# Two attention and two feed-forward layers on one core: the K weights loaded in two column halves, the first K products split to match, and a new order

## The chip, the cores and the metric

The kernel runs on one core of one Trainium2 chip. The metric is the device time of one execution in microseconds. A profiled execution has a span, from its first to its last instruction, and a device time a little longer than that. The engines are TensorE (PE, with its weight loads shown apart as PEld), VectorE (DVE), ScalarE (ACT), GpSimd (POOL) and SyncE (SP), which issues all the DMAs here.

## The reference

The input x has 2048 rows of 512. Four residual layers follow: attention, feed-forward, attention, feed-forward, the two of each kind with the same weights.

```python
x = x + attn(layernorm(x), wqkv, wo)
x = x + ffn(layernorm(x), w1, w2)
x = x + attn(layernorm(x), wqkv, wo)
x = x + ffn(layernorm(x), w1, w2)

# attn: 32 heads of 16
q, k, v = split(x @ wqkv)
phi = lambda t: where(t > 0, t + 1, exp(t)) + 1e-6
kv  = einsum("bhsd,bhse->bhde", phi(k), v)
z   = einsum("bhsd->bhd", phi(k))
o   = (phi(q) @ kv) / (phi(q) . z + 1e-6)
out = o @ wo

# ffn: relu(x @ w1) @ w2, with 1376 hidden columns
```

## The kernel before

The 2048 rows are 16 tiles of 128 rows (one row per partition), and four tiles make a chunk. A layer's input is normalised tile by tile into `xn` (float16) and transposed into `Tb`, so that the 512 columns lie on partitions, in four blocks of 128. A K product of a tile (`kproj`, function `a_k`, L653) is four matmuls, one for each block, each 512 columns wide, into one PSUM bank; ACT then makes an exponential and a linear copy of it, and DVE joins the two to phi(k) (`phi_evac`, L610). A Q product is made transposed, four per chunk. For chunk 0 of layer 0 it is made in halves of two tiles, 256 columns wide (`a_q_half`, L735), and the evacuation follows the second half. G products (`a_g`) multiply xn with phi(k) over all rows; from G come the value part, the denominators and the matrix that the chunk's last products (`fin`) use. The feed-forward layers replace some products by sums and differences of blocks.

In layer 0, tiles of chunks 0 and 1 are transposed on PE (`transpose_pe`, L591: four 128-wide matmuls against an identity, then a copy to `Tb` on ACT or DVE); all the others are transposed by DMA, two tiles at a time (L586). The statistics of layer 0's tiles are made by DVE (L534, L535), the reciprocal root by ACT (tiles 0 to 3) or POOL, and the normalised tile by DVE (L572). From tile 2 on the statistics of a tile wait for the normalised tile two before it.

Before there is any input, PE runs eight matmuls on zeros (L503, `warm`). Behind the transposes of tiles 0 and 1 it runs four more each (`warm_fill`, L525 and L529), 128 columns wide; nothing reads their result.

All loads are issued by SP on one hardware queue, in the order of their priorities. Before: tile 0 of x, tile 1, tiles 2 and 3, wk (columns 512 to 1023 of wqkv, all 512 rows), chunk 1 of x, wq (columns 0 to 511), chunk 3, chunk 2, wv, one row of wv, wo, w1; w2 later. All chunks but the first few rows are read so that a partition holds consecutive rows.

The order of everything is planned by the program itself while it is built. Every operation is added to a graph with an assumed duration (`C_MM512` = 216 and so on) and, for a DMA, an assumed transfer time and lateness (`late`). `_list_schedule` (L200) then goes through the engines, each with a window of pending operations sorted by priority, and places the one that can start first. The priority is the operation's place in the program plus a number from the table `HINTS` (L55). An entry ending in `!` fixes which of several engines makes the operation. PSUM banks are handed out by the same planner. The order that comes out is written out as the instruction streams, each engine's in order, with semaphore waits where another engine or a DMA is waited for. The planner's times are only used to choose the order.

Steps of consecutive layers are interleaved: the next layer's step for a chunk begins as soon as its rows are ready, and the matmuls of both stand in one PE stream.

Of the kernel before, what the change touches and what calls it, by code (L numbers as in the profile page):

```python
# [16 lines left out]
C_MM512 = 216.0  # L17
# [37 lines left out]
HINTS = {"0.bnag8": 129, "0.bnst11": -246, "0.bnst12": 104, "0.bnst13": 129, "0.bnst14": 143, "0.bnst15": 144, "0.bnst6": -4,  # L55
# [276 lines left out]
def build_kernel(nc, A_x, A_wqkv, A_wo, B_w1, B_w2, out, n_layers_pairs=2, K_STT=0, Q_STT=0, windows=None,  # L332
# [20 lines left out]
    with es:  # L353
# [237 lines left out]
        def transpose_pe(i):  # L591
# [11 lines left out]
            if i < 2:  # L603
                warm_fill(i)
# [781 lines left out]
```

## Time and profile before

| | |
|---|---|
| median of 3 runs | 269.01 us (268.01 to 269.33) |
| profiled execution | 268.93 us, span 267.2 us |
| granted TensorE clock over the span, as recorded | 1.0 |
| PE busy | 262.0 us, 98% |
| DVE busy | 226.2 us, 85% |
| ACT busy | 187.0 us, 70% |
| POOL busy | 58.5 us, 22% |
| DMA | 22.18 MB, mean 83 GB/s |

In the profile L12 is line 12 of the kernel. A line of the chain gives start, length and what it was. A line of the timeline gives the start and the time from the first start to the last end of a run of like instructions (x4 is four of them), the engine, the line, the operation, what it writes and reads by the program's names, and its shape; in brackets the idle time before it and what ended that. PE rows include the drain of a matmul, which the next one overlaps, so a row of four matmuls is longer than four intervals. "DMA to landing" is the time from a DMA's issue to its completion.

### The profile page before, as it was taken

The page shows a single profiled execution, that of the slowest core. Times are in us where ns is not written, and L with a number is a line of the kernel's source. Part 1 is how long each engine was busy: PE and PEld are TensorE (multiplying, and loading weights), DVE is VectorE, ACT ScalarE, POOL GpSimd, SP SyncE. Part 2 cuts the span into 40 slices and gives each one's busy share as a digit, 9 for nine tenths or more (in the row PEclk, how much of TensorE's full clock was granted, in tenths as well). Part 3 has the DMA queues.
Part 4 walks back from the last instruction along what each step waited for, and adds up shares of the span by engine and source line. Part 5 has one row for each costly group of instructions (what it writes and reads, how often), then busy time and mean ns, then how long its engine had stood idle before and what let it go on. Part 6 is the DMA issues. An engine that isn't in the chain of part 4 may idle for free.

```text
span 267.2 us, 5481 instructions
## 1 busy us (share of the span) xinstructions
PE 262.0 (98%) x2020; PEld 183.1 (69%) x2020; DVE 226.2 (85%) x636; ACT 187.0 (70%) x408; POOL 58.5 (22%) x146
## 2 busy tenths in 40 slices
PE   7999999999989999999999999999999999999995
PEld 3664547644745798857768755674488789888884
DVE  5799974789888999997998675459999999899994
ACT  4998896766975237999667797787899936057400
POOL 3210000026682001403103430000744434000000
PEclk9999999999999999999999999999999999999999
DMA  7986620763765000400400421054373223402003
GB/s 205 368 285 137 197 42 3 157 146 65 86 120 98 2 20 2 89 11 2 79 2 0 79 54 28 2 129 108 62 153 68 39 39 101 81 0 72 28 34 126
DMA packets 44890, 22.18 MB, mean 83 GB/s; under 512 B 34784, under 2 KB 43328, under 8 KB 44864
## 3 DMA queue, kind: packets, MB, share of 16 engines
q1 hardware_dynamic: 44864, 21.83, 34.3%
q8 instruction: 16, 0.26, 0.4%
q14 instruction: 10, 0.08, 0.1%
HBM read 7.14 MB, written 2.10 MB: 35 GB/s over the span
## 4 chain that ended last, share of the span: by engine, by line
PE 92%; ACT 3%; DMA 3%; DVE 1%; SPq 0%; issue 0%; DVEq 0%
PE ps L635 91%; ACT sqscr L650 2%; DMA Tb<-xn 2%; DMA xin<-in_A_x_dram 1%; PE ps L600 1%; ACT xn L581 1%; DVE xres L642 0%; DVE bst L534 0%; PE ps L529 0%; DVE rdc L1064 0%; SPq L471 0%; DVEq L1324 0%; DVE xn L572 0%; ACT big L946 0%
## 5 line engine op out<-in xcount | busy, mean ns | idle before, releaser
L618 ACT ACTIVATE big<-ps 128x512 bf16<-128x512 f32 x64 | 40.7, 644 | 9.5 <-PE ps L635 9.4
L650 ACT ACTIVATE sqscr<-xres 128x512 bf16<-128x512 f32 x48 | 30.0, 625 | 9.1 <-DVE xres L642 5.1
L635 PE MATMUL ps<-Tb,w 128*128 128x256 f16 (+1 forms) x216 | 35.3, 304 | 0.0
L635 PE MATMUL ps<-w,big 128*128 128x256 bf16 (+1 forms) x256 | 32.4, 272 | 0.0
L635 PE MATMUL ps<-wqkv,Tb 128*128 128x512 bf16 x128 | 31.2, 379 | 0.0
L635 PE MATMUL ps<-big,xn 128*128 128x256 bf16 (+1 forms) x224 | 31.1, 288 | 0.0
L635 PE MATMUL ps<-Tb,wqkv 128*128 128x512 f16 (+1 forms) x144 | 30.8, 355 | 0.0
L620 ACT ACTIVATE escr<-ps 128x512 bf16<-128x512 f32 x48 | 29.6, 634 | 1.1 <-PE ps L635 1.1
L635 PE MATMUL ps<-Mf,big 128*128 128x512 bf16 x128 | 29.6, 379 | 0.0
L635 PEld LDWEIGHTS ps<-w,big 128*128 128x128 bf16 (+1 forms) x256 | 24.9, 98 | 3.6 <-ACT big L946 0.3
L635 PEld LDWEIGHTS ps<-big,xn 128*128 128x128 f16 x224 | 21.3, 98 | 8.5 <-issue 0.8
L635 PEld LDWEIGHTS ps<-Tb,w 128*128 128x128 bf16 x216 | 20.6, 98 | 8.8 <-DMA Tb<-xn 0.4
L908 ACT ACTIVATE escr<-ps 128x512 f32<-128x512 f32 (+1 forms) x40 | 20.3, 544 | 8.1 <-PE ps L635 7.4
L895 DVE TENSOR_TENSOR big<-ps,escr 128x512 bf16<-128x512 f32 (+1 forms) x40 | 23.6, 603 | 1.7 <-ACT escr L908 1.1
L564 POOL TENSOR_TENSOR rstd<-veps,nhalf 128x2 f32<-128x2 f32 x24 | 20.4, 853 | 7.9 <-DVE veps L562 6.8
L635 PEld LDWEIGHTS ps<-Tb,wqkv 128*128 128x128 bf16 x144 | 13.7, 98 | 11.7 <-ACT escr L620 0.3
L635 PEld LDWEIGHTS ps<-Mf,big 128*128 128x128 bf16 x128 | 12.3, 98 | 13.8 <-ACT Mf L717 0.2
L622 DVE TENSOR_SCALAR escr<-escr 128x512 bf16<-128x512 bf16 x48 | 13.7, 289 | 8.6 <-ACT escr L620 8.4
L635 PEld LDWEIGHTS ps<-wqkv,Tb 128*128 128x128 f16 x128 | 12.2, 98 | 12.4 <-ACT Tb L606 0.4
L628 DVE TENSOR_TENSOR big<-big,escr 128x512 bf16<-128x512 bf16 x48 | 19.8, 419 | 0.8 <-ACT big L618 0.2
L581 ACT ACTIVATE xn<-xres,nbias,rstd 128x512 f16<-128x512 f32 x21 | 16.8, 815 | 5.1 <-DVE nbias L566 3.9
L898 ACT ACTIVATE big<-big 128x512 bf16<-128x512 bf16 (+1 forms) x31 | 16.2, 542 | 4.8 <-DVE big L895 4.7
(116 smaller groups left out, 515.9 us busy)
## 6 DMA issues: line engine op xcount, KB each, us to landing
big<-rdc SPq DMA_DIRECT2D x32, 128.0 KB, 2.7
wqkv<-in_A_wqkv_dram SPq DMA_DIRECT2D x3, 512.0 KB, 7.0
xin<-in_A_x_dram SPq DMA_DIRECT2D x3, 512.0 KB, 7.8
w<-in_B_w_dram SPq DMA_DIRECT2D x1, 1376.0 KB, 14.5
w<-in_B_w_dram SPq DMA_DIRECT2D x1, 1280.0 KB, 7.0
wo<-in_A_wo_dram SPq DMA_DIRECT2D x1, 512.0 KB, 10.3
out_dram<-GT SPq DMA_DIRECT2D x1, 512.0 KB, 4.1
out_dram<-Mf SPq DMA_DIRECT2D x1, 512.0 KB, 2.6
```

The costliest lines, as they stand in the source:

```text
L564: g.add(POOL, lambda e: e.tensor_tensor(rstd[:, sl], veps[:, sl], nhalf[:, 0:n], ALU.pow), [("veps", lo), ("nhalf",)], [("rstd", i) for i ...
L581: (ACT, lambda e: e.activation(xn[:, i, :], src, ACTF.Identity, scale=rstd[:, i:i + 1], bias=nbias[:, i:i + 1]), C_ACT_SB_AP)],
L600: last = e.transpose(psb()[:, 128 * c:128 * c + 128], xn[:, i, 128 * c:128 * c + 128], ident[:])
L618: g.add(ACT, lambda e: e.activation(dst_ap, psv[:, b, :], ACTF.Identity, bias=1.0 + 1e-6, scale=1.0), [("ps", b)], [dst_key], C_ACT_PSUM, ...
L620: g.add(ACT, lambda e: e.activation(sap, psv[:, b, :], ACTF.Exp), [("ps", b)], skeys, C_ACT_EXP, name=name + "_exp")
L622: g.add(DVE, lambda e: e.tensor_scalar(sap, sap, 1.0, 1e-6, ALU.min, ALU.add), skeys, skeys, C_DVE_BF4X, name=name + "_em")
L628: g.add(DVE, lambda e: e.tensor_tensor(dst_ap, dst_ap, sap, ALU.max), [dst_key] + skeys, [dst_key], 340.0, name=name + "_phi")
L635: last = e.matmul(o, l, r, start=st, stop=sp, skip_group_check=skip)
L650: g.add(ACT, lambda e: e.activation(sqscr[:, q, :], xres[:, i, :], ACTF.Square, scale=math.sqrt(INV_D), accum_out=s2[:, i:i + 1]), xr(i), ...
L895: g.add(DVE, lambda e: e.tensor_tensor(ap, sh(psv[:, bank, 0:w]), sh(other()), ALU.add), [("ps", bank)] + okeys + ([] if first else bk), q ...
L898: g.add_flex([(ACT, lambda e: e.activation(ap, ap, ACTF.Relu), C_ACT_PSUM if len(cs) == 2 else 270.0), (DVE, lambda e: e.tensor_scalar(ap, ...
L908: g.add(ACT, lambda e, w=w: e.activation(q[:, 0:w], psv[:, bank, 0:w], ACTF.Identity), [("ps", bank)], key, C_ACT_PSUM if len(cs) == 2 els ...
```

## The change

wk is loaded in two DMAs of 256 columns each, `wka` and `wkb`. The program's order of the loads is now: tile 0, tile 1, wka, tiles 2 and 3, wkb, wq, chunk 1, the rest as before; with the new priorities that is also the order of their issue. So tiles 2 and 3 of x have half of wk ahead of them, and chunk 1 has wq ahead of it.

The K products of tiles 0 and 1 in layer 0 are made in two groups of four matmuls, 256 columns wide, into the two halves of the same bank: the first needs wka only, the second wkb. All other K products are unchanged and name both loads. The filler behind the transposes of tile 1 is dropped; the one behind tile 0 stays. The assumed transfer time of a weight load goes by its columns, and the assumed lateness of wka, wkb, and tiles 2 and 3 is 650 ns (before, 500 for wk and 200 for the tiles). The table `HINTS` is replaced as a whole, so the planner's order differs in all four layers, and so do its choices of engine.

```diff
-HINTS = {"0.bnag8": 129, "0.bnst11": -246, "0.bnst12": 104, "0.bnst13": 129, "0.bnst14": 143, "0.bnst15": 144, "0.bnst6": -4,
+HINTS = {"0.bnag0": 160, "0.bnag12": 230, "0.bnag4": 31, "0.bnag8": 144, "0.bnst11": 122, "0.bnst12": -78, "0.bnst13": 213,
...
-                350.0 * (hi - lo), "ld_x%d" % lo, issue=C_LOAD_ISSUE, late={1: 100.0, 2: 200.0}.get(lo, C_LATE))
+                350.0 * (hi - lo), "ld_x%d" % lo, issue=C_LOAD_ISSUE, late={1: 100.0, 2: 650.0}.get(lo, C_LATE))
...
         def ld_w(sl, key):
-            dma(lambda e: e.dma_start(wqkv[:, :, sl], wq_v[:, :, sl]), [], [(key,)], 1480.0, "ld_" + key, issue=C_LOAD_ISSUE, late=500.0 if key == "wk" else C_LATE)
+            dma(lambda e: e.dma_start(wqkv[:, :, sl], wq_v[:, :, sl]), [], [(key,)], 2.9 * (sl.stop - sl.start), "ld_" + key, issue=C_LOAD_ISSUE, late=650.0 if key[:2] == "wk" else C_LATE)
...
         ld_x(1, 2)
-        ld_w(slice(D, 2 * D), "wk")
+        ld_w(slice(D, D + 256), "wka")
         ld_x(2, 4)
+        ld_w(slice(D + 256, 2 * D), "wkb")
         ld_w(slice(0, D), "wq")
...
-        ALL_LOADS = [("wk",), ("wq",)]
+        ALL_LOADS = [("wka",), ("wkb",), ("wq",)]
...
-            if i < 2:
+            if i < 1:
                 warm_fill(i)
...
-        def a_k(i):
+        def a_k(i, first_k=False):
             b = alloc_bank()
-            mm_group(lambda: [(psv[:, b, :], Tb[:, i, c, :], wqkv[:, c, D:2 * D], c == 0, c == 3, False) for c in range(4)],
-                     [("T", i), ("wk",)], [("ps", b)], 4 * C_MM512, "kproj%d" % i)
+            if first_k and i < 2:
+                for h, key in enumerate(("wka", "wkb")):
+                    mm_group(lambda h=h: [(psv[:, b, 256 * h:256 * h + 256], Tb[:, i, c, :], wqkv[:, c, D + 256 * h:D + 256 * h + 256],
+                                           h == 0 and c == 0, c == 3, True) for c in range(4)],
+                             [("T", i), (key,)], [("ps", b)], 4 * C_MM256, "kproj%d_%d" % (i, h))
+            else:
+                mm_group(lambda: [(psv[:, b, :], Tb[:, i, c, :], wqkv[:, c, D:2 * D], c == 0, c == 3, False) for c in range(4)],
+                         [("T", i), ("wka",), ("wkb",)], [("ps", b)], 4 * C_MM512, "kproj%d" % i)
             phi_evac(b, pk_tile(i), ("big", pk_unit(i)), "k%d" % i, stt=(i % 4) < K_STT)
...
-                        a_k(i)
+                        a_k(i, first_layer)
```

119 rows, old and new, of the table HINTS are left out of this document.

## The prediction

> **What bounds the kernel now.** I read the page first (busy shares, the chain that ended last), then the chain piece by piece, the waits of PE, and the timeline of the first 15 us, where all the named edits lie. The page and the chain:
>
> ```profile
> span 267.2 us, 5481 instructions
> ...
> PE 262.0 (98%) x2020; PEld 183.1 (69%) x2020; DVE 226.2 (85%) x636; ACT 187.0 (70%) x408; POOL 58.5 (22%) x146
> ```
>
> ```profile
> 19.69 43.25 PE ps L635 x264
> ...
> 71.85 4.67 DMA Tb<-xn
> 76.51 0.05 issue
> 76.56 187.63 PE ps L635 x1544
> 264.19 0.02 issue
> 264.21 0.42 DVE rdc L1064
> ```
>
> The reader is to see that PE is the bound, nearly without holes: 43 us and then 188 us of the chain are matmuls back to back. PE is idle for 267.2 - 262.0 = 5.2 us: 1.24 before the first warm matmul, 3.0 at the end (264.2 to 267.2: last DVE sum and its store), and about 1 us in between, nearly all in one wait:
>
> ```profile
> PE ps L503 <- DVE wrm L496: 1.2, 1, 1.2
> PE ps L635 <- DMA Tb<-xn: 0.8, 1, 0.8
> ```
>
> Busy time hides short gaps (a matmul row includes its drain), so I also took the starts of successive matmuls and subtracted the usual interval (216 ns for 512 columns, 109 for 256, 57 for 128). What remains after the warm-up is 0.99 us at 75.35 (the 0.8 of the waits above, plus a drain), 0.13 at 113.8, 0.12 and 0.07 near 193, all at transposes of a new layer's input; 0.26 before the second transpose, 0.11 and 0.11 in the first ten microseconds; and about 0.5 each time the denominators' 32-column matmuls begin and end. An order or a load can win only from these: at most 1.3 at the layer changes and about 0.5 at the start. The start:
>
> ```profile
> 4.96 0.61 PE L600 MATMUL ps<-ident,xn 128*128 128x128 f16 x4
> 5.37 0.63 PE L529 MATMUL ps<-wrm 128*128 128x128 bf16 x4
> 5.61 0.60 ACT L606 ACTIVATE Tb<-ps 128x512 f16<-128x512 f16 x1
> 6.00 0.56 PE L600 MATMUL ps<-ident,xn 128*128 128x128 f16 x4
> 6.40 0.39 PE L529 MATMUL ps<-wrm 128*128 128x128 bf16 x4
> 6.60 0.60 ACT L606 ACTIVATE Tb<-ps 128x512 f16<-128x512 f16 x1
> 6.73 1.04 PE L635 MATMUL ps<-wqkv,Tb 128*128 128x512 bf16 x4
> ```
>
> ```profile
> L470 SPq DMA_DIRECT2D wqkv<-in_A_wqkv_dram x3: 434/443/707, 2.2 to 5.1; - x3
> ...
> DMA to landing us min/median/max: 4.5/7.0/9.1
> ```
>
> The two fillers (L529) stand while PE waits; the first K product (L635) starts at 6.73. Of the three weight loads wk is the first, issued at 2.18, and lands 4.5 later, at 6.69: it, not tile 0 (copied by 5.61 + 0.60 = 6.21), releases that product. wq, issued at 3.20, lands 7.0 later, at 10.15, and Q products start at 10.80. The individual landings are x of tile 1 at 3.88, tiles 2 and 3 at 4.81, wk 6.69, chunk 1 at 8.66, wq 10.15. Beside PE, the other engines have little room there:
>
> ```profile
> 6.00:12.00 6.00, 6.00 (x43) 3.63 (x44) 4.49 (x17) 5.61 (x15) 1.00 (x3) 1.00 1.00 376
> 12.00:18.00 6.00, 6.00 (x50) 4.28 (x48) 5.93 (x18) 6.00 (x14) 1.50 (x3) 1.00 1.03 346
> 18.00:24.00 6.00, 6.00 (x41) 3.39 (x39) 6.00 (x25) 5.25 (x14) 0.12 (x1) 1.00 0.44 105
> ```
>
> After the stretch the columns are its length, then PE, weight loads, DVE, ACT and POOL busy, granted clock, DMA share, GB/s. From 6 to 14 us the DMA share is 1.0: loads queue on the transfer, not on the issue.
>
> **The change part by part.** *First K product.* With the first half of wk in place it needs the copy of tile 0 (6.21) and PE free of the second transposes (6.00 + 4 x 0.10 = 6.40). So 6.40 in place of 6.73: 0.33 gained. Filler 1 ran from 6.40 to 6.63 inside that wait; its removal is worth nothing by itself, and lets the half start there. The half takes 4 x 0.109 = 0.44, to 6.84. The second half waits for wkb: the bytes up to it are those up to wk before, so 6.69 at the same rate. The rows become 512 B instead of 1 KB; in the trace's packet records a 1 KB packet of the loads took 46 ns, a 512 B packet of the last stores 27.7, so 512 KB over 16 engines is 64 x 27.7 = 1.77 us against 32 x 46 = 1.47: 0.30 later, 6.99. Bounds of the gap: 0 to 0.2; I take 0.1, the middle. Product 0 then ends at 7.38, not 7.61: 0.23 gained. What queues behind that wait on PE is product 1 and the transposes of tile 2, and ACT waits for both halves before its exponential.
>
> [...]
>
> *More, smaller matmuls.* Two K products become 16 x 0.109 = 1.74 us in place of 8 x 0.216 = 1.73: +0.02. Eight more weight loads of 98 ns run beside matmuls. The one more load is an issue of 0.43 on SP's queue; loads are issued by 7.3 but land by 21.8, so the transfer hides it.
>
> *x of tiles 2 and 3 behind wka.* 256 KB more ahead of it: 4.81 becomes about 5.7. DVE is in norm 1 until 5.95, so its statistics slip by 1 us from 4.94: 5.95 + 0.69 + 0.17, Ln and Exp behind ACT's copy of tile 1 (to 7.60), norm 0.41, xn at about 8.05. PE is in K product 1 (0.87) until 8.25: covered by 0.2. The copy to Tb (0.60) is not: it ends near 9.1, and PE needs the Q half products of tiles 0 and 1 (16 x 0.109 = 1.75) as cover.
>
> *wq ahead of chunk 1.* wq goes to 6.69 or 6.99 plus 1.5 to 2.0 (what wq and chunk 1 took), 8.2 to 9.0, against PE free at 8.47: gap 0 to 0.5. I take 0.1, since the nearer row (1.49 for this load) gives no gap. If wq is later still, PE idles.
>
> *Chunk 1 behind wq.* It lands at about 10.2 to 10.5 instead of 8.66; its statistics, which began at 9.29, begin 0.9 to 1.2 later. From there to T of tile 4 took 5.0 us (9.29 to 14.28); the bare chain (0.69 + 0.17 + 0.15 + 0.65 + 0.41 + 0.39 + 0.60, and 0.3 of handing over) takes 3.4. So 13.6 to 15.5, with PE wanting it at about 14.4. Cost: 0 to 1.1; I take 0: DVE idles for 1.5 of the 6 us before 12 and can finish K's work while it waits.
>
> *The new order.* Every priority and engine choice of all four layers is drawn anew; PE's work is the same. It moves only the waits at layer changes (0.99, 0.13, 0.19). Bounds: all gone, -1.3; or a K-sized group of cover less (4 x 0.216 = 0.87) at each of the three, +2.6. I take -0.3: the largest drawn back to the mean of the three, 0.44 (-0.55), the two small ones growing a little (+0.25). Tail and denominators: 0, between one fewer switch (-0.5) and one more (+0.5).
>
> Sum, on the profiled execution's 268.93 (span 267.2 plus 1.7 around it): -0.23 + 0.10 + 0.02 - 0.30 = -0.41, so 268.5; that execution lies 0.08 below the median of 269.01, so 268.6 as a median.
>
> **The rivals.**
> *Both waits go* (faster). K starts at 6.40 and neither wkb nor wq leaves a gap (-0.33), and the transposes at all three layer changes come in time (-1.3): 269.01 - 1.6 = 267.4. For it: the one large wait is single, its cover only 1 us short. Against: every one of the four has to go.
> *Chunk 1 starves* (no gain). The T of tile 4 comes at 15.5 and tile 5 follows at DVE's pace: +1.1 - 0.2: 269.9, inside half a per cent. For it: DVE and ACT are full from 12 on. Against: G products of chunk 0 are ready to fill in from 15.6 on.
> *Less cover at a layer change* (slower). The transposes of a layer's first chunks are issued one after another on SP (1.2 to 2.6 us each) and land 3 to 5 us later; PE runs on other products meanwhile. The new order places one group of 0.87 less ahead of them at each change: 3 x 0.87 = 2.6, less 0.4, 271.2. It decides from two such groups on (1.7 - 0.4 = 1.3). For it: ACT is full from 66 to 72, ahead of the 0.99 wait. Against: two of three changes wait for under 0.2 now.
> *The clock comes later* (slower). Warm matmuls of 512 columns start 427 ns apart, later ones 216; the switch lies between 6.30 and 6.40, where transposes go from 107 to 56 apart. If less PE work around 6 us puts it off, K and Q run at half speed meanwhile. The chance is small: what is removed lies behind the switch, and a K half takes its place. [...]
> [...]
>
> **How the numbers follow.** Half a per cent, 1.35 us, is about what a measurement of this kernel can tell from no change. Forecast 0.40 (its own range 267.9 to 269.2); both waits go 0.17; chunk 1 starves, or the halves buy nothing, 0.16; less cover 0.22; the clock 0.05. Faster needs 1.35 of the 1.8 there are: 0.17. Slower has no floor: 0.27. Same: 0.56. The range reaches from just below the first rival to just below the slowest, 267.1 to 271.0.
>
> **What would show it.** First K product at 6.4 and its second half at 6.8 to 7.1; Q half products near 8.5; tile 4's K product by 14.5; no idle PE over 0.3 before 40; the wait for DMA transposes under 0.8. The prediction is wrong if PE's waits at layer changes sum to over 2.5 us or vanish, or if PE stands idle around 10 to 20 us.

## The result and the profile after

The changed kernel takes 271.25 us in the median of 6 runs (270.39 to 272.7), the kernel before 268.89 beside it. The ratio is 1.0091, 95% interval [1.0063, 1.012]: slower by 2.4 us, where I had forecast 268.6 and set 271.0 as the upper end. The profiled execution took 271.71 us (before: 268.93), span 270.0 (before: 267.2).

The page of the changed kernel, engines and one DMA queue that matters later:

```profile
span 270.0 us, 5489 instructions
...
PE 262.1 (97%) x2024; PEld 183.7 (68%) x2024; DVE 223.0 (83%) x626; ACT 189.2 (70%) x412; POOL 58.8 (22%) x152
...
q8 instruction: 16, 0.26, 0.5%
```

PE's busy time is what it was (262.0 before), and the span is 2.8 us longer: the new time is idle time of PE. The waits of PE name it; the columns are the sum, the number of waits and the longest:

```profile
PE ps L643 <- DMA Tb<-xn: 2.2, 2, 1.5
PE ps L511 <- DVE wrm L504: 1.2, 1, 1.2
PE ps L643 <- DMA wqkv<-in_A_wqkv_dram: 0.6, 2, 0.4
PE ps L608 <- DVE xn L580: 0.5, 1, 0.5
PE ps L643 <- DVE big L785: 0.3, 1, 0.3
```

Before there was only the second of these and 0.8 for one DMA transpose. The chain that ended last shows where they lie (start, length, what):

```profile
3.20 6.71 DMA wqkv<-in_A_wqkv_dram
9.96 4.52 PE ps L643 x32
...
51.76 4.11 DMA big<-rdc
56.46 1.04 PE ps L643 x4
...
72.13 4.85 DMA Tb<-xn
77.03 97.11 PE ps L643 x740
...
192.97 4.70 DMA Tb<-xn
197.72 69.26 PE ps L643 x654
```

Before, PE's matmuls ran from 76.56 to 264.19 without a break. Now the chain leaves PE at four places: for wq at 9.96, for a copy of `rdc` near 56, for the transpose that already cost time before (77), and for a transpose near 197. The timeline of the first ten microseconds, and the row of the last of the four:

```profile
4.83 0.73 DVE L580 TENSOR_SCALAR xn<-xin,mv,rstd 128x512 f16<-128x512 bf16 x2 [0.37 <-ACT rstd L550]
5.30 0.35 PEld L608 LDWEIGHTS ps<-ident,xn 128*128 128x128 f16 x4 [1.37 <-DVE xn L580]
...
6.60 0.80 PE L643 MATMUL ps<-wqkv,Tb 128*128 128x256 bf16 x4
...
7.80 1.49 PE L643 MATMUL ps<-wqkv,Tb 128*128 128x256 bf16 x12 [0.41 <-DMA wqkv<-in_A_wqkv_dram]
...
9.96 0.72 PE L643 MATMUL ps<-Tb,wqkv 128*128 128x256 f16 x5 [0.22 <-DMA wqkv<-in_A_wqkv_dram]
...
197.72 0.85 PE L643 MATMUL ps<-w,Tb 128*128 128x96 bf16 x16 [1.54 <-DMA Tb<-xn]
```

The first transposes start at 5.30 (before: 4.96), because the new order lets DVE finish the statistics of tiles 0 and 1 before it normalises tile 0. The first K half starts at 6.60, the second half waits for wkb, which lands at 7.76, and the Q halves wait for wq, which lands at 9.91.

As in the prediction I also took the starts of successive matmuls and subtracted the usual interval. After the warm-up, the places over 0.3 us are: 0.57 at 7.13 (wkb), 0.38 at 9.52 (wq), 0.47 at 55.77, 0.85 at 76.13, 1.71 at 195.90; together 3.98, against 0.99 before. The same sum over all the profiled executions below gives a simple reading: device time less these waits is 266.7 to 267.9 us for thirteen of them, before and after included (271.71 - 3.98 = 267.7; 268.93 - 0.99 = 267.9). The fourteenth, in which the clock fell, is told below. So whatever the change does to the amount of work lies within that spread of 1.2 us; the waits decide, and the experiments ask where they come from.

### The profile page after: what moved, and what is told of

Its sections match the earlier page's. It is cut to its first block, busy times and chain, and to the rows that moved or that the text cites. A ratio compares the mean times of both kernels' runs of the same rounds, so it can differ in the third digit from the quotient of the medians.

```text
span 270.0 us, 5489 instructions
## 1 busy us (share of the span) xinstructions
PE 262.1 (97%) x2024; PEld 183.7 (68%) x2024; DVE 223.0 (83%) x626; ACT 189.2 (70%) x412; POOL 58.8 (22%) x152
## 4 chain that ended last, share of the span: by engine, by line
PE 75%; DMA 9%; DVE 6%; ACT 4%; SPq 4%; issue 1%; DVEq 0%
PE ps L643 75%; DVE xres L650 4%; DMA Tb<-xn 4%; SPq L779 3%; DMA big<-rdc 3%; DMA wqkv<-in_A_wqkv_dram 2%; ACT sqscr L658 1%; DVE big L785 1%; ACT lnd L767 1%; ACT xn L589 1%; ACT rdc L769 1%; PE ps L608 0%; DVE xn L584 0%; SPq L472 0%; SPq L477 0%
## 5 line engine op out<-in xcount | busy, mean ns | idle before, releaser
L626 ACT ACTIVATE big<-ps 128x512 bf16<-128x512 f32 x64 | 38.6, 622 | 5.9 <-PE ps L643 5.8
L643 PE MATMUL ps<-wqkv,Tb 128*128 128x512 bf16 (+1 forms) x136 | 31.4, 368 | 0.4 <-DMA wqkv<-in_A_wqkv_dram 0.4
L643 PEld LDWEIGHTS ps<-wqkv,Tb 128*128 128x128 f16 x136 | 13.1, 99 | 12.7 <-DMA wqkv<-in_A_wqkv_dram 0.7
L589 ACT ACTIVATE xn<-xres,nbias,rstd 128x512 f16<-128x512 f32 x20 | 15.8, 808 | 7.5 <-DVE nbias L574 5.7
L1062 DVE TENSOR_TENSOR xres<-ps,xres 128x512 f32<-128x512 f32 x24 | 16.3, 684 | 4.0 <-PE ps L643 4.0
```

The source lines that it names most:

```text
L589: (ACT, lambda e: e.activation(xn[:, i, :], src, ACTF.Identity, scale=rstd[:, i:i + 1], bias=nbias[:, i:i + 1]), C_ACT_SB_AP)],
L626: g.add(ACT, lambda e: e.activation(dst_ap, psv[:, b, :], ACTF.Identity, bias=1.0 + 1e-6, scale=1.0), [("ps", b)], [dst_key], C_ACT_PSUM, ...
L643: last = e.matmul(o, l, r, start=st, stop=sp, skip_group_check=skip)
L1062: g.add(DVE, lambda e: e.tensor_tensor(dst, psv[:, bank, :].rearrange("p (a k) -> p a k", k=256), dst, ALU.add), [("ps", bank)] + keys, ke ...
```

## The experiments

Two theories were set against each other. **Loads:** the second half of wk, in 512 B rows and behind the x of tiles 2 and 3, comes late, and wq behind it. **Fetches:** PE's instructions come in blocks by DMA too (queue q8 in the page: 16 blocks, 0.26 MB, so 16 KB each, one for about 250 matmuls and weight loads), and in the changed kernel these blocks fall where a transpose or a copy is just needed. What led to the second: of the transpose issued at 192.97, the landing records of 15 of its 16 parts lie from 195.97 to 196.11, that of the last at 197.67; the copy issued at 51.76 has 15 parts by 54.42 and the last at 55.87. In both stretches one such block was under way (at 195.65 and 53.1). The DMA view of the changed kernel from 192 to 198 us (packets, MB, share of 16 engines):

```profile
q1 hardware_dynamic: 2256, 0.66, 56.0%
q8 instruction: 1, 0.02, 1.0%
```

1.0% of 16 engines for 6 us is 0.96 us of one engine, for one block. The change moves these blocks too: it has 8 PE instructions more (2024 matmuls against 2020, each with its weight load).

| run | what | median us (its before) | ratio, 95% interval |
|---|---|---|---|
| after | the change | 271.25 (268.89) | 1.0091 [1.0063, 1.012] |
| r1 | the change once more | 270.92 (268.80) | 1.0083 [1.0057, 1.0109] |
| r2 | the change, 78 PE instructions more in the warm-up | 269.33 (268.80) | 1.003 [1.0002, 1.0057] |
| r3 | before, the same 78 | 268.69 (268.80) | 0.9987 [0.9962, 1.0011] |
| r4 | the change with before's priorities | 274.07 (268.80) | 1.0187 [1.0137, 1.0237] |
| r5 | before, wq ahead of chunk 1 | 269.23 (268.71) | 1.002 [0.999, 1.005] |
| r6 | before, wk and two K products in halves | 270.15 (268.71) | 1.0058 [1.0029, 1.0087] |
| r7 | the change, wk whole | 269.89 (268.71) | 1.0042 [1.0016, 1.0067] |
| r8 | before, 52 PE instructions more | 269.02 (268.71) | 1.0018 [0.9991, 1.0046] |
| r9 | r7 and r2 together | 268.97 (268.56) | 1.0033 [1.0004, 1.0062] |
| r10 | the change, norm of tile 0 first | 270.47 (268.56) | 1.007 [1.0043, 1.0096] |
| r11 | r9 and r10 together | 268.78 (268.56) | 1.0017 [0.9989, 1.0045] |
| r12 | before, 22 PE instructions more | 268.74 (268.86) | 0.9991 [0.9973, 1.001] |

**r1, the change once more.** No edit.

> The changed kernel once more, unchanged, for a second trace of it. Theory F (PE's own instruction fetches, 16 KB each on one DMA engine, hold up the last sixteenth of a transpose or a copy that PE then waits for): the wait of 1.7 us near 196 and the 0.5 near 55.8 are there again, each with a fetch in the 2 us ahead and one of 16 landings 1 us or more behind the others, since a fetch comes after a fixed count of PE instructions. Theory O (the new order gives too little cover there): the waits are there, whatever one landing does. Rival C (chance of one execution): they are gone or half as long. Start: second half of the first K product at 7.8 again if it belongs to the loads, under 7.1 if one slow landing was chance. Time 271.2, ratio 1.009 for all.

The loss is there again. In its profile (269.79 us, its fastest run) wkb landed at 6.98 and wq at 9.03, with waits of 0.30 and 0.28; the wait at 75 was 0.86, and there was one of 0.82 for a transpose at 201.77. At 194.55 only 0.13 was lost: the transpose there landed all its parts from 194.54 to 194.74. The 1.71 of the first profile is thus not there in every execution, though program and order are the same. Single waits of one profile must not be added up as if they were the median.

**r2, PE's instructions moved against its work.** The warm-up runs 45 small and 2 large matmuls instead of 8 large, so the same real work comes 78 PE instructions later in PE's stream, and if the blocks go by the count of instructions they come that much sooner against it; the order of the real work is kept. In the profile of r2 no block was under way from 188 to 196 us, where the change had one at 195.65 and r1 one at 194.08.

```diff
-                for k in range(WARM):
-                    last = e.matmul(psv[:, wt, :], wrm[:, 0:128], wrm[:, :], start=True, stop=True)
+                for k in range(45):
+                    last = e.matmul(psv[0:64, wt, 0:64], wrm[:, 0:64], wrm[:, 0:64], start=True, stop=True)
+                for k in range(2):
+                    last = e.matmul(psv[:, wt, :], wrm[:, 0:128], wrm[:, :], start=True, stop=True)
```

> The changed kernel with all orders kept; only the matmuls on zeros ahead of the first input are 45 of 64x64 and 2 of 128x512 in place of 8 of 128x512. That puts 78 more instructions (39 weight loads, 39 matmuls) ahead of everything on PE in the same time, so each later fetch comes 78 PE instructions earlier: near 189 in place of 195.65, 69 in place of 74.5, 48.6 in place of 53.1. Theory F: the wait near 196 falls from 1.7 to under 0.4, that near 55.8 from 0.5 to 0.1, the one near 76 from 0.85 to 0.4 or less; time 271.2 - 1.5 to 2.2 = 269.0 to 269.7. Theory O (order, too little cover): all waits as before, 271.2 within 0.3.

1.6 us of r1's 2.1 are gone (medians 270.92 and 269.33 on the same chip). PE's waits of r2:

```profile
PE ps L511 <- DVE wrm L504: 1.2, 1, 1.2
PE ps L645 <- DMA wqkv<-in_A_wqkv_dram: 0.7, 1, 0.7
PE ps L645 <- ACT lnd L924: 0.6, 1, 0.6
PE ps L610 <- DVE xn L582: 0.5, 1, 0.5
PE ps L645 <- ACT Tb L616: 0.2, 1, 0.2
```

The waits at 55.8, 76 and 196 are gone, and wq's stays (0.88 between matmuls; it landed at 9.47). So does the one near 201: 0.72 at 201.3, for 0.82 in r1. The view puts it down to ACT, but the transpose that these matmuls read landed at 202.03, and PE went on at 202.17.

**r3, the same in the kernel before.** It tells whether the other warm-up is faster by itself.

> The kernel before with the same 78 instructions ahead. Its fetch at 71.75 lay amid the transposes whose landing ended PE's wait of 0.99 at 75.35. Theory F: that wait falls under 0.3; the fetch near 194.3 goes to 187.6; time 268.9 - 0.8 = 268.1 (ratio 0.997), unless a moved fetch hits another transpose. Theory O: wait and time unchanged, 268.9 within 0.3.

It is not: 0.9987. The old wait at 75 is gone, and a new one of 1.23 stands at 88.65, where a transpose issued at 85.41 had 15 parts at 87.96 and the last at 89.94, with a block under way from 87.9. In before, moving the blocks exchanges one such wait for another.

**r4, the change without its new order.** The table of priorities is that of before; only the entries that name loads are as in the change. The planner makes a new order from it, which differs from that of before in the start.

```diff
-HINTS = {"0.bnag0": 160, "0.bnag12": 230, "0.bnag4": 31, "0.bnag8": 144, "0.bnst11": 122, "0.bnst12": -78, "0.bnst13": 213,
+HINTS = {"0.bnag8": 129, "0.bnst11": -246, "0.bnst12": 104, "0.bnst13": 129, "0.bnst14": 143, "0.bnst15": 144, "0.bnst6": -4,
...
```

> All the named edits of the change (wk in halves round tiles 2 and 3, wq ahead of chunk 1, first K products in halves, one filler less), with the priorities of before in place of the new table (the loads alone keep the new priorities). The order that comes out is that of before from about 45 us on and differs only in the start. If the new order alone is to blame for the loss: 268.9 or a little less (0.997 to 1.000). If late loads are (second half of wk at 7.8, wq at 9.9): chunk 0 ends 0.8 to 1.3 later than before and 270 (1.003 to 1.005). Theory F: the counts of PE instructions are 8 up by the halves and 8 down by the filler, so the fetch near 71.7 meets the transposes as before and that wait stays at 0.8 to 1.0.

Far worse: 1.0187. The windows of this run (after the stretch: its length, then PE, weight loads, DVE, ACT and POOL busy, granted clock, DMA share, GB/s):

```profile
12.00:16.00 4.00, 4.00 (x32) 2.73 (x32) 3.73 (x12) 3.36 (x8) 1.08 (x2) 1.00 1.09 376
16.00:20.00 4.00, 2.46 (x13) 0.84 (x12) 4.00 (x17) 4.00 (x10) 1.08 (x2) 1.00 0.76 292
20.00:24.00 4.00, 2.94 (x10) 1.23 (x11) 3.02 (x11) 3.66 (x9) 0.12 (x1) 0.57 0.01 2
```

PE starves from 17 to 24 us (waits of 1.17 for DVE's normalised tile, 1.15 and 0.78 for the copies to Tb), and after two of them the granted clock falls to half for 3.41 us, from 20.46. This is the slowest of six executions; one other of them has the clock of this one (0.994), and the four at 1.0 still take 272.0 to 274.1. It looks like the "chunk 1 starves" of the prediction, but that chunk 1's place behind wq is to blame is not shown: r5 below has the same place in the order of before and no such wait. In r4 PE also has no G product to fill in before 25.3 us, while r5 and the change run theirs from 16.0 and 16.6. In the same loads the new order has no wait over 0.3 us between 10 and 55 us, so it bears them where the order planned from the old priorities does not.

**r7, the loads alone taken back.** In the change, wk comes whole again behind tiles 2 and 3, in 1 KB rows; wq stays ahead of chunk 1, the K products of tiles 0 and 1 stay in halves, and the order of every compute engine is kept.

```diff
+        order[SP].remove(by["ld_wkb"])
+        first = ["ld_x0", "ld_x1", "ld_x2", "ld_wka", "ld_wq", "ld_x4"]
+        order[SP][:len(first)] = [by[n] for n in first]
...
+            em = slice(D, 2 * D) if key == "wka" else sl
+            dma(lambda e: e.dma_start(wqkv[:, :, em], wq_v[:, :, em]), [], [(key,)],
...
```

Here `ld_wka` loads all of wk.

> The changed kernel with every engine's order kept, K products of tiles 0 and 1 still in halves; wk is loaded whole again, with 1 KB rows, behind tiles 2 and 3, and wq still ahead of chunk 1. If the 512 B rows and the lagging landing of the second half cost the start: wk lands at 6.4 to 6.7, no wait between the halves, wq at 8.3 to 9.0, chunk 1 at 10.0, PE's loss by 20 us is 0.3 to 0.8 less, time 270.3 to 270.6. If the loss comes from the order of the statistics (both tiles' statistics ahead of the first norm) and from wq: 271.0 as the change.

1.0042: 0.9 us of 2.1 go (1.18 over before, against r1's 2.12). PE's timeline of this run:

```profile
5.22 0.40 PE L609 MATMUL ps<-ident,xn 128*128 128x128 f16 x4 [0.39 <-DVE xn L581]
...
6.63 1.91 PE L644 MATMUL ps<-wqkv,Tb 128*128 128x256 bf16 x16 [0.56 <-DMA wqkv<-in_A_wqkv_dram]
8.37 0.61 PE L609 MATMUL ps<-ident,xn 128*128 128x128 f16 x8
8.82 1.47 PE L644 MATMUL ps<-Tb,wqkv 128*128 128x256 f16 x12
```

wk landed at 6.49, all sixteen K half products run without a gap and end at 8.37, wq landed at 8.26 and nothing waits for it. By then PE has the two K products and, 8 x 0.057 later, the transposes of tiles 2 and 3 behind it: at 8.83. In before the same work is done at 8.92 (8.69 + 4 x 0.057), in the profile of the change at 9.59 (9.13 + 0.46). So the new start with wk whole wins 0.1 us, and in that one profile the split of the load turns it into a loss of 0.7. The other profiles of the change's loads and order reach this point at 8.80 (r1), 8.64 (r2) and 9.15 (r10), so in the mean of the four the split costs 0.2 up to here. The Q halves behind it, which wait for wq, start at 9.08 to 9.98 in these four, and at 8.82 in r7.

Farther on, r7 keeps the waits of the change: 0.86 at 54.55 (again for a copy whose last part is late: 15 parts by 53.17, the last at 55.03, a block from 52.83), 0.69 at 75.30 and 0.78 at 202.2.

```profile
PE ps L644 <- DMA Tb<-xn: 1.1, 2, 0.6
PE ps L644 <- DVE big L786: 0.7, 1, 0.7
```

**r5 and r6, parts of the change put into before.** In both the order of every compute engine is that of before. r5 only issues wq ahead of chunk 1; r6 loads wk in halves round tiles 2 and 3 and makes the two K products in halves, with chunk 1 ahead of wq and both fillers.

```diff
+        first = ['ld_x0', 'ld_x1', 'ld_x2', 'ld_wk', 'ld_wq', 'ld_x4']
...
+        first = ['ld_x0', 'ld_x1', 'ld_wk', 'ld_x2', 'ld_wkb', 'ld_x4', 'ld_wq']
...
+        order[SP][:0] = [by[n] for n in first]
```

The first of these lines is r5's, the second r6's, the last stands in both.

> The kernel before with every engine's order kept; SP alone issues wq ahead of chunk 1 of x. Theory L (chunk 1's late landing is the price of the change: DVE and ACT then run out of time for tiles 4 to 7): chunk 1 lands at 10.1 in place of 8.7, the transposes of tile 4 come 0.9 to 1.5 later, PE waits between 10 and 25 us, and the time goes up by 1 to 3 us, 270 to 272. Rival (the wait is hidden, DVE idles for 1.5 us there anyway): under 0.5, 269.

> The kernel before with every engine's order kept; wk comes in two column halves round tiles 2 and 3, the K products of tiles 0 and 1 are in halves, chunk 1 stays ahead of wq, both fillers stay. If the halves do what they say: first K product at 6.63 (behind filler 1), second half by 7.1 if all sixteen parts of wkb land together, by 7.8 if one lags; transposes of tile 2 at 8.1 in place of 7.6. The loss by 10 us is then 0.3 to 0.8, the rest as before: 269.1 to 269.6 (1.001 to 1.003). If the split gains: under 268.8.

r5: 1.002, no difference that can be measured, and after the first K product no wait over 0.3 us until 75: wq (8.56) ahead of chunk 1 (9.84) costs nothing that can be measured here (the interval reaches 1.3 us). r6: 1.0058, so the halves cost 1.4 us in the old order, more than the 0.3 to 0.8 that I expected from the start alone. Its timeline of PE:

```profile
6.62 0.40 PE L602 MATMUL ps<-ident,xn 128*128 128x128 f16 x4 [1.11 <-DVE xn L574]
...
8.14 0.61 PE L663 MATMUL ps<-wqkv,Tb 128*128 128x256 bf16 x4 [0.47 <-DMA wqkv<-in_A_wqkv_dram]
```

The old order on DVE has the statistics of tile 2 ahead of the normalised tile 1, so x of tiles 2 and 3, landing at 5.45 (5.42 in the profile of r5, where it cost 0.95; 4.81 in before), holds up the second transposes; and wkb landed at 8.10. PE also waits 1.24 at 192.86 in this profile, for a transpose issued at 189.98 that landed at 194.27, with a block under way from 191.1 to 192.3. The halves put 16 PE instructions more into the stream, so in r6 the blocks move as well (this one from 194.28 in before), so it is not certain that the 1.4 us come from the loads alone. The profiled r5 (271.04, its slowest run) has, in the order of before, the very wait that made me suspect the new order: 1.77 at 195.20, for a transpose whose parts landed from 195.36 to 195.50 and the last at 197.03, with a block fetched from 195.0. PE's waits there:

```profile
PE ps L635 <- DMA Tb<-xn: 2.5, 2, 1.6
```

**r8, before with 52 instructions more.** The warm-up as in r2, with 30 small and 4 large matmuls.

> The kernel before with 52 more PE instructions ahead (30 matmuls of 64x64 and 4 of 128x512 in place of 8). Theory F: the fetches go to 69.0 to 69.6 and 88.8 to 89.2, clear of the transposes at 70.4 to 75 and of the one at 86.6 to 88.5 that the shift by 78 hit, so that neither the wait of 0.99 at 75 nor the one of 1.23 at 88.65 is there: 268.0 (0.997). Rival (waits at layer changes are a matter of the order): a wait of 0.5 or more at 75.

1.0018, again no difference, where the fetch theory had forecast 0.997. 0.42 at 53.3 and 0.62 at 153.3 came in place of the wait at 75, besides 0.76 at 6.37 for wk, which landed at 6.91. The 0.62 is for a transpose that took 4.35 us from issue to landing, with a block under way from 151.2 to 152.1: here too the shift exchanged one meeting for another.

**r9, r10, r11: do the parts add up?** r9 joins the edits of r7 and r2. r10 puts the normalised tile 0 ahead of the last statistics step of tile 1 on DVE and ACT, in the changed kernel; r11 does that in r9.

```diff
+        seq = ["bnst0", "bnag0", "lnv0", "bnst1", "rstd0", "norm0", "bnag1", "lnv1", "rstd1", "norm1"]
```

> The kernel after with two edits: wk is loaded whole again, behind tiles 2 and 3, with wq still ahead of chunk 1 and the order of every compute engine kept; and PE's warm-up is 45 small and 2 large matmuls, 78 PE instructions more, which moves every later fetch of PE's instructions earlier. If the late second half of wk and the meeting of instruction fetches with transposes are two separate costs (the ratio fell from 1.0083 to 1.0042 by the first edit alone and to 1.003 by the second alone), the two gains add up: a ratio near 0.999, some 268.5 us, with no wait over 0.3 us between the first K product and 25 us and none at 55, 76 or 196. If they overlap, or if the moved fetches meet other transfers, it stays at 1.002 to 1.004, some 269.5 us.

> The kernel after, with VectorE and ScalarE doing the norm of tile 0 ahead of the last step of tile 1's statistics, as in the kernel before; nothing else moves. The first transposes should start near 4.96 instead of 5.30 us. If that delay of 0.34 us counts, the ratio falls by 0.001, to 1.007. If the K products wait for the second half of wk and the Q products for wq in any case, what is gained ahead of them is waited for behind, and the ratio stays at 1.008.

> The run with wk whole and the warm-up of 78 PE instructions more, and the norm of tile 0 ahead of the last step of tile 1's statistics besides. Here no half of wk is late, so if the delayed norm counts anywhere it counts here: 0.3 us below that run, a ratio near 0.998. If wk, landing at about 6.5 us, sets the start of the K products in both, the two runs agree within 0.2 us.

They do not add up. r9 is at 1.0033, where the sum of the two gains would have been 0.999: what is left above before is 0.4 us, as in r2 (0.5). With the blocks moved, wk in halves or whole makes no difference that can be measured; without, it makes 0.9, where both intervals reach 0.7 us to either side. In the profile of r9 wq landed at 9.95, late by one slow packet, and cost 1.21, more than in any run with halves. How much of r7's gain was the start and how much another meeting with the blocks stays open. The norm is worth 0.2 us both times (1.91 over before against r1's 2.12; 0.22 against r9's 0.41), less than the intervals, so likely but not shown. In r10 the first transposes start at 4.85 and the first K half at 6.15, and PE then waits 0.78 for wkb and 0.83 for wq: what is won ahead is waited for behind. The rest of this profile (271.71, its slowest run) repeats that of the change: 0.56 at 55.8, 0.72 at 76.3 and 1.72 at 195.9, the first with a block from 53.3 and 15 parts of the copy by 54.49 and the last at 56.01, the third with a block from 195.6 and 15 parts of the transpose by 196.08 and the last at 197.66.

```profile
PE ps L643 <- DMA Tb<-xn: 2.1, 2, 1.6
```

r11 reaches before within the interval (1.0017); PE's waits in its profile (268.70 us):

```profile
PE ps L512 <- DVE wrm L505: 1.2, 1, 1.2
PE ps L646 <- DMA Tb<-xn: 0.7, 1, 0.7
```

This is the new order with wk whole, the norm first and the blocks moved: as good as before, not better. No combination beat before. The 0.7 (0.81 between matmuls) is the wait near 201 again. It stands in all five profiles of the new order in which PE was not already 1.7 late there (0.82 in r1, 0.72 in r2, 0.78 in r7, 0.76 in r9), while no profile with the old priorities has a wait for this transpose. Its parts land together, 3.3 to 3.4 us after the issue, and no block is under way. So this wait is the new order's own. In before the same transpose landed at 201.84, 0.2 us ahead of its matmuls.

**r12, a test of the fetch theory by forecast.** If a meeting with a block is what costs, I should be able to make before slower by a bad shift. By the trace of before, 22 PE instructions more put blocks 1 to 3 us behind the issue of five transposes.

> The kernel before with nothing changed but PE's warm-up: 12 small and 7 large matmuls instead of 8 large, which is 22 PE instructions more (78 in one earlier run of it, 52 in another). By the trace of before, the fetches of PE's instructions then start near 34.6, 52, 70.6, 152.8, 193.2 and 204.8 us, each 1 to 3 us behind the issue of a transpose (32.2, 69.1, 149.9, 191.8 and 203.6 us), closer to the distances of 2.4 and 2.7 us at which the kernel after lost 0.85 and 1.71 us. If it is these meetings that cost time, this shift is a bad one, where 78 was harmless: new waits of 0.5 us or more for a transpose or for a late copy in one or more of those places, and a ratio of 1.003 to 1.008, some 269.5 to 270.8 us. If the transposes have enough time in hand there, or if a fetch only costs where something else is late too, the ratio stays within 0.999 to 1.002.

On time it failed: 0.9991. PE's waits in the profile of r12 (270.10, its slowest run):

```profile
PE ps L637 <- DMA wqkv<-in_A_wqkv_dram: 1.3, 1, 1.3
PE ps L503 <- DVE wrm L496: 1.2, 1, 1.2
PE ps L637 <- DMA Tb<-xn: 0.9, 2, 0.7
```

The blocks came at 37.7, 53.5, 71.5, 153.3, 190.9 and 206.7, half a microsecond to 3 us from where I had put them, so the test is weaker than it was meant to be. Only one transfer there shows a late last part (a transpose of `hr` issued at 204.75: 15 parts by 207.17, the last at 209.10), and nobody waited for it. The 0.91 at 193 belongs to a transpose all of whose parts landed together, but 3.89 us after its issue, with the block of 190.9 to 192.2 in between; without one they take 3.1. So a new wait of over 0.5 did come where I had forecast one, in this profile, and the median does not show it. The largest wait, 1.49 between matmuls at 6.24, is for wk, which landed at 7.75, and has nothing to do with the blocks, the first of which came at 17.3. Distances alone do not tell which part a block holds up, nor whether PE needs it then.

**What the fourteen profiles show together.** Of 504 transposes issued after 20 us, 97 had a block under way between issue and landing. Of these, 31 took over 4 us; of the other 407, none did (median 3.06). Of all 1092 transfers issued after 20 us, 188 met a block, and in 32 of them the last part landed over 0.7 us behind the 15th; in the other 904 that never happened.

The packet records show how. The transpose issued at 192.97 in the change ends with 32 packets of 4 bytes. Of these, 30 had started by 195.54, the block ran from 195.65 to 196.59, and the last two packets started at 196.58 and 196.59; the late part landed 1.07 us later. In all nine transposes with a late last part two such packets start within 0.03 us of the block's end. In the wait at 76 the block (74.53 to 75.46) met the transpose in its middle: hardly a packet of it started meanwhile, then one came every 0.03 us until 76.2, while 20 others, begun before the block ended, lasted 1.6 to 2.0 us and ended together at 76.3. The DMA view of 72.2 to 77 us in slices of 0.12 us:

```profile
GB/s 226 218 207 220 207 198 192 181 165 77 171 211 235 213 226 188 203 194 171 190 4 0 0 0 0 0 0 9 9 9 11 9 11 49 182 0 0 0 0 0
q8 instruction: 1, 0.02, 1.2%
```

The five profiles with 52 or 78 instructions more (r2, r3, r8, r9, r11) have no wait between 70 and 85 us; the other nine have one of 0.33 to 1.07 there. In r1 the block came at 194.08 amid the 32 packets, all had started by 194.19, and nothing was late.

## Why the prediction was wrong

**What bounds it.** Right: PE is the bound and only waits move the time. The floor of 266.7 to 267.9 under thirteen profiles shows it better than I had. The steps that said work costs nothing (smaller matmuls +0.02, one filler less, one load more) stand: r7 and r11 have all of these and no wait over 0.3 us between the K products and 54 us.

**First K product, -0.33 and 0.1 for wkb.** The step failed, more in the second number than in the first. The product started at 6.60, not 6.40. I had taken the row of tile 0's copy (6.21) from the trace of before, while the new order delays its normalised tile by 0.3; the hint for `bnag0` in the diff says so, and I costed the order only at layer changes. But in r1 and r2, whose clock was at full speed from 5.00 and 4.94 on (7.02 in the first profile), the same order starts the product at 6.28 and 6.35; and r10, which undoes the delay, is 0.2 better, within the intervals. And wkb was to land at 6.69 to 6.99, by packets: 15 of its 16 parts did (6.84). The last came at 7.76, and in the other profiles with halves wkb landed at 6.98, 6.76, 7.33, 7.80 and 8.10; in the last two the 15th part was as late (7.78 and 7.66). PE waited 0 to 0.88 for it. Whole, wk landed from 6.34 to 7.10 in seven of eight profiles, at 7.75 in one. I had the usual price of a packet right (medians of 27 ns for 512 B in this load, 46 for 1 KB) and left out that a load is there when its slowest part is. The packet rows had the smaller rows as the slower ones: 512 B in 27 ns is 19.0 GB/s within a packet, 1 KB in 46 is 22.3.

**wq ahead of chunk 1, +0.10.** Mis-sized in the change: wq landed at 9.91 (9.03 to 9.93 in the other runs of the change's loads), beyond the 9.0 of my bound, and cost 0.28 to 0.88. With wk whole it lands at 8.2 to 8.6 in three profiles of four, as I had it, and costs nothing; in the fourth, r9, one slow packet put it at 9.95, and it cost 1.21. So the halves seem to be behind this term too; five profiles against four are few.

**x of tiles 2 and 3, chunk 1.** The costs, 0 and 0, were right in the changed kernel: x at 5.87 for 5.7, covered; chunk 1 at 11.19, later than my 10.5, and tile 4's K product at 15.74 for 14.5, and still PE did not wait. The rival that I priced at 1.1 may be what r4 shows, with 5.3 us: its four executions at full clock lost 3.2 to 5.3, and in two of six (granted clock 0.994) a phase at half speed came on top, 3.41 us in the profiled one, which I had not counted.

**The new order, -0.30.** This is the step that carried the forecast, and it failed. I let the largest wait shrink to 0.44; it stayed (0.99 before, 0.85 after, 0.86 in r1), and others came at places that had none or little: up to 1.71 near 196, 0.47 to 0.86 for the late copy near 55, and 0.72 to 0.82 near 201. At the layer changes I had forecast 1.0 in place of 1.31; it was 2.6 in the first profile, 2.4 in r10 and 1.8 in r1. By r2 about 1.6 us of the loss goes when PE's instruction blocks are moved and the real work is not. With the loads mended, the norm first and the blocks moved, the new order is level with the old within the interval (r11, 0.2 above): about 0, not -0.30. I had priced the order by how much work it puts in front of a transpose. That holds for the wait near 201 alone. Around 190 to 197 the two kernels' orders are nearly the same, shifted by 1.1 us, and the wait differs by 1.6: the transpose took 4.70 us there in place of 3.09, which I had no term for.

**The rivals.** "Less cover at a layer change", 271.2, came out in time, by luck more than in kind. One of its three waits is there, 0.72 to 0.82 near 201 for 0.87; the larger one near 196, and that near 76, which before has too, are not for want of matmuls in front but for a transpose that a block held up. That a rival with 0.22 lay just outside the range was a mistake by itself; a range that reaches 271.2 needed only 0.2 more. "The clock comes later": in the changed kernel's profile the switch is at 7.02 (6.39 before), and the first K half ran at half speed for part of it, but r1 has it at 5.00, so it is no feature of the change.

**What is shown and what is open.** Shown: a block of PE's instructions that comes while a transpose is under way can hold up two of its closing packets, or, in its middle, all of it; it then lands 1 us and more late (4.85 us after its issue near 76, 4.70 near 196, where the median without a block is 3.06), and in the changed kernel PE then waits 0.85 near 76 and up to 1.71 near 196. Moving PE's instruction stream by 78 takes 1.6 us off the change and nothing off before. The new order has a wait of 0.7 to 0.8 of its own near 201, bears the new loads, and wins nothing. The halves, with the 16 PE instructions that they add, cost 1.4 us in the old order. Less sure: the 0.9 us that they cost in the change, which is not there once the blocks are moved, and that wq first is free by itself, which the interval of r5 leaves open up to 1.3 us. Not shown: that block and late part share one of the 16 DMA engines; the trace does not name the engine, though packets that start as a block ends say so strongly. Open: which meetings cost time (66 of 97 transposes that met a block took no more than 4 us), and why the median of the change suffered so much more than before did at four positions. r5's profile shows that the old order too can lose 1.77 in one execution, and both forecasts of a time from block positions alone, r8 and r12, missed.

## What to carry to other kernels

When a kernel has almost no idle time, a new order of equal work can, as here, mostly redraw which transfers come late: compare it at two or three offsets of the instruction stream (a few idle matmuls more at the start) before you credit or blame the order itself. Price a split load by its slowest part (the last of wkb landed 0.92 us behind the 15th) and by everything queued behind it, not by its mean rate. And take waits from several profiles: the same program lost 1.71 us at one place in one execution and 0.13 in the next.

## What the runs showed of the hardware

Blocks of PE's instructions are transfers like others: 16 of 16 KB in each run, the first between 12 and 19 us, one for about 250 matmuls and weight loads (212 to 282 from the start of one to the next in the profiles of before and after), each recorded as one packet of 0.9 to 1.7 us. By their starts the count is thus not as fixed as the expectation of r1 has it. Of 97 transposes that met a block 66 took no more than 4 us. But 31 took longer, of 407 that met none not one did, and where PE needed such a transpose it waited 0.6 to 1.8 us.

Single packets of the loads sometimes took far longer than their kind: one of 1 KB in wq took 1.69 us in r9 (median 46 ns) and put wq at 9.95, two of 4 KB took 1.26 and 1.29 us in the profile after. What holds them up, the trace does not tell; no block was under way yet.

The clock's switch to full speed was recorded between 4.5 and 7.0 us, and the full-speed phase lasted 262.83 us in most runs, 266.24 in one, which is 3.41 more. r4's phase at half speed lasted 3.41 as well. r4 shows the way back too: waits of 1.17 and 1.15 us, 0.2 us apart, were followed by that phase at half speed. A single wait of 1.7 to 1.8 us, near 196 to 200 in four profiles, was not.
